# Retention and gated unit on one core: value weights behind a third unit of loads, first gated units a turn later, loads behind the stores

## Chip, cores and metric

The kernel runs on one core of a Trainium2 chip. The metric is the device time of one execution in microseconds (us), less is better. The five engines of the core are TensorE (PE), VectorE (DVE), ScalarE (ACT), GpSimd (POOL) and SyncE (SP); each works through its own instructions in order, and transfers between HBM and the on-chip memory SBUF are issued from the queues of SP, ACT or POOL.

## What is computed

A retention layer (attention without softmax, with a decay) feeds a gated unit: a causal convolution of five taps gives a gate, a projection gives values, and their product is projected again. There are 8 batches, 8 heads, 576 positions, 64 elements per head; everything is given and returned in float32.

```python
scores = q @ k.T / sqrt(64)                       # [8, 8, 576, 576]
ret = scores * gamma_h ** (s - t)                 # where s >= t, else 0
x = (ret @ v), heads side by side                 # [8, 576, 512]
gate = sigmoid(sum_k conv_w[k] * x[s - 4 + k])    # per channel
out = (gate * (x @ w_val)) @ w_out                # [8, 576, 512]
```

## The kernel before

The decay is split into a factor for the key's position (`gin`, put into v when it is cast to bf16) and one for the query's position (`gout`, put into the result), so that a state of 64x64 per head can be carried along the sequence instead of the full score matrix.

The work is cut into 18 units (`dcs`, L68 to L72): for each group of four batches eight "full" units of 256 positions (two per batch) and one "tail" unit that holds the last 64 positions of the four batches. Unit 8 and unit 17 are the tails. The loads of q, k and v for a full unit are one DMA of 512 KB each (L87); for a tail they are four DMAs of 128 KB each (L92), with pieces of 256 bytes, so twelve in all.

The main loop (L506) goes over m = 1 to 18. The order of instructions on each engine is written out by hand in it. Turn m does the scores, masks, state update and result of unit m, and beside it the later stages of earlier units: the convolution and gate of unit m-1 (`conv` L390, `gate` L405), the value projection of unit m-1 (`value` L410, in two halves i) and the output projection of unit m-2 (`project` L420, in two halves i). It also transposes q and k of unit m+1 (`turn`, copied from PSUM by ACT in `take_turned`, L271), casts k, q and v of unit m+2 to bf16 on GpSimd (L225, L241), and issues the loads of unit m+6. Unit 0 is done in a prologue (L451 to L501), where the loads of units 0 to 6, the weights and the masks are prepared as well.

What the steps below touch:

- Buffers for loaded q, k, v: four each (`ld`, LB = 4), so the load of unit m+6 needs the cast of unit m+2 done.
- `ob` (L426): the SBUF tile from which an output half is stored, five buffers. `project` copies PSUM to `ob` on ACT (L432) and issues the store on SP (L434). A copy waits until the store five copies ago has landed.
- `ps_g`: two PSUM banks that conv, value, project and others take in turn. A matmul into a bank waits until what was in it has been read.
- SP's queue holds nearly all loads and all stores in program order. In turn m: store of project(m-2, 0), loads of unit m+6, store of project(m-2, 1).
- Value weights `wvf` (L106): four DMAs of 256 KB, each into 64 of the 128 partitions (L112), issued after the loads of units 0 and 1. `prep_wv` (L213) casts them into the order of columns that `ORDER` (L121) gives, in two parts: part 1 on GpSimd in the prologue, part 0 on ACT in m=1.
- Output weights `wob` (L122): four DMAs from GpSimd's queue, each into 64 partitions, converted to bf16 on the way (L127).
- `dg`: four diagonals (one per block of channels) made by `prep_diagonals` (L209) from the convolution weights, which `prep_conv_weights` (L201) transposes into `cw`. All four are made on VectorE, at four places.
- `keep_warm` (L444): matmuls on zeros that keep TensorE occupied.

Of the kernel before, what the change touches and what calls it, by code (L numbers as in the profile page):

```python
# [21 lines left out]
def kernel(  # L22
# [57 lines left out]
    with tc.manual_schedule():  # L80
# [14 lines left out]
        def load(name, m):  # L95
            t = ld.tile([P, H, R, D], F32, name=f"f{name}")
            fetch(nc.sync, t, {"q": q, "k": k, "v": v}[name], m)
            loaded[name, m] = t

        cwn = consts.tile([KC * NP, P], F32, name="cwn")  # L100
        nc.scalar.dma_start(out=cwn, in_=moe_conv_w.rearrange("k (o i) -> (k o) i", i=P))
        for m in range(2):
            for name in "kqv":
                load(name, m)

        wvf = consts.tile([P, NP, DM], F32, name="wvf")  # L106
        wv_src = moe_w_val.rearrange("(op ob hl i) n -> ob hl i op n", ob=2, hl=2, i=HP)
        wv_dst = wvf.rearrange("p (op ob) n -> ob p op n", ob=2)

        def load_wv(eng, i):  # L110
            for ob in range(2):
                eng.dma_start(out=wv_dst[ob, half[i]], in_=wv_src[ob, i ^ ob])  # L112

        for i in range(2):
            load_wv(nc.sync, i)
        for m in range(2, LB):
            for name in "kqv":
                load(name, m)


        ORDER = ((0, 0, 1, 0), (HP, 0, 0, 1), (0, 2, 0, 0), (HP, 2, 1, 1))  # L121
        wob = consts.tile([P, NP, DM], BF16, name="wob")  # L122

        def load_wo():
            src = moe_w_out.rearrange("(pr ab hl p) n -> ab hl p pr n", pr=2, ab=2, hl=2)
            for (p0, blk, ab, hl) in ORDER:
                nc.gpsimd.dma_start(out=wob[p0:p0 + HP, blk:blk + 2, :], in_=src[ab, hl])  # L127


        zeros = consts.tile([P, DM], BF16, name="zeros")  # L130
# [4 lines left out]
                                compare_op=ALU.is_equal, fill=0.0)  # L135
        idb = consts.tile([P, HP], BF16, name="idb")
        nc.vector.tensor_tensor(idb, ident[:, 0:HP], ident[:, HP:P], op=ALU.add)
        toki = consts.tile([P, NCH + 1, R], mybir.dt.int32, name="toki")
        nc.gpsimd.iota(toki[:, 0:NCH], pattern=[[W, NCH], [1, R]], base=0, channel_multiplier=R)
        nc.gpsimd.iota(toki[:, NCH], pattern=[[0, R]], base=NCH * W, channel_multiplier=1)  # L140
# [42 lines left out]
            if pr == 1:  # L183
                nc.scalar.activation(gin, gin, AF.Exp)
        warm = consts.tile([P, 1], F32, name="warm")
        identf = consts.tile([32, 32], F32, name="identf")
        nc.vector.tensor_copy(identf, ident[0:32, 0:32])
        id2 = consts.tile([P, HP], F32, name="id2")
        nc.vector.tensor_copy(id2, idb)

        xg = [[xp.tile([P, GB, NP, PAD + (W if c < NCH else TAIL)], BF16, name=f"x{g}{c}") for c in range(NCH + 1)]
              for g in range(B // GB)]
# [8 lines left out]
        def prep_conv_weights():  # L201
            cps = spare(ps_g, "g")[:, 0:KC * NP]
            nc.tensor.transpose(cps, cwn, identf[0:KC * NP, 0:KC * NP])
            cps = cps.rearrange("p (k o) -> p k o", k=KC)
            nc.vector.tensor_copy(cw[:, :, 0::2], cps[:, :, 0::2])
            for i in range(2):
                nc.vector.tensor_copy(cw[half[1 - i], :, 1::2], cps[half[i], :, 1::2])

        def prep_diagonals(o, eng):  # L209
            eng.tensor_tensor(dg[:, o], cw[:, :, o].unsqueeze(2).to_broadcast([P, KC, HP]),  # L210
                              id2.unsqueeze(1).to_broadcast([P, KC, HP]), op=ALU.mult)
# [18 lines left out]
        def cast_k(m, *copies):  # L230
            cast("k", m, copies)
# [25 lines left out]
        def turn(which, m, bank=None):  # L257

            src = (kbf, qbf)[which][m]
            dst = new_bank() if bank is None else bank  # L260
            for pr in range(NP):
                for r in range(R):
                    nc.tensor.transpose(dst[:, pr, r, :], src[:, pr, r, :, :].rearrange("p i d -> p (i d)"), ident)  # L263
            return dst
# [125 lines left out]
        def conv(n):  # L390

            g = [ps_g.tile([P, 2, 2 * P], F32, name="g") for _ in range(2)][::-1]
            gps[n] = g
            gsb[n] = {}
            lists = [], []
            for pr in range(2):
                a, b = 2 * pr, 2 * pr + 1
                for kk in range(KC):
                    for bank, rows, blks in ((0, half[1], (b, a)), (1, half[0], (a, b))):
                        lists[bank].append([mm(g[bank][half[i], pr, :], lhsT=dg[rows, blks[i], kk, :],  # L400
                                               rhs=xs(n, rows, blks[i], kk), start=(pr == 0 and kk == 0),
                                               stop=(pr == 1 and kk == KC - 1)) for i in range(2)])
            return lists
# [37 lines left out]
        ok = lambda m: 0 <= m < ND  # L441
        v_copy, g_copy, s_copy = nc.vector.tensor_copy, nc.gpsimd.tensor_copy, nc.scalar.copy

        def keep_warm(n):  # L444

            t = ps_o.tile([P, NP, R, HP], F32, name="o0").rearrange("p o r n -> p (o r n)")
            for _ in range(n):
                nc.tensor.matmul(t, zeros[:, 0:P], zeros, start=True, stop=True)  # L448


        keep_warm(8)  # L451
        cast_k(0, (v_copy, 4))
        bank = turn(0, 0)
        take_turned(0, 0, bank, (v_copy, 4))
        cast_q(0)
        prep_conv_weights()
        prep_diagonals(0, nc.vector)
        keep_warm(3)
        bank = turn(1, 0, spare(ps_g, "g", [P, NP, R, P], BF16))
        take_turned(1, 0, bank, (s_copy, 2), (v_copy, 2))  # L460
# [4 lines left out]
        for m in range(LB, LB + 2):  # L465
            for name in "kqv":
                load(name, m)
        prep_wv(g_copy, 1)
        keep_warm(3)
        run(scores(0, 0))  # L470
        masks(0, 0, 0)
        masks(0, 0, 1)
# [3 lines left out]
        keep_warm(2)  # L476
        run(update(0, 0))
        take_state(0, 0)
        keep_warm(1)
        run(update(0, 1))  # L480
        take_state(0, 1)
        run(carried(0, 1))
        prep_diagonals(1, nc.vector)
        prep_diagonals(2, nc.vector)
        bank = turn(0, 1)
        take_turned(0, 1, bank)
        bank = turn(1, 1)
        take_turned(1, 1, bank)
        run(*values(0, 1))
# [2 lines left out]
        take_x(0, 0)  # L492
        take_x(0, 1)
        pass_on(0)
        for (name, f) in (("k", cast_k), ("q", cast_q)):
            f(2)
            load(name, LB + 2)
        load_wo()
        cast_v(2)
        load("v", LB + 2)  # L500
        prep_diagonals(3, nc.vector)  # L501

# [1 line left out]
        for m in range(1, ND + 1):  # L506
            now, nxt, last = ok(m), ok(m + 1), m == ND
            late = m < 4
            hi, lo = conv(m - 1)

            if now:
                run(scores(m, 0))
                masks(m, 0, 0)
                masks(m, 0, 1)
            if last:
                run(lo, hi)
                gate(m - 1, 1)
                gate(m - 1, 0)
            elif late:
                run(lo[0:8], hi[0:8])  # L520
                run(pairs(update(m, 0)), hi[8:10])
                take_state(m, 0)
                gate(m - 1, 0)
                run(pairs(update(m, 1)), lo[8:10])
                take_state(m, 1)
                gate(m - 1, 1)
                run(carried(m, 1))
            else:
                run(carried(m, 1))
                run(pairs(update(m, 1)), lo[0:2])  # L530
                take_state(m, 1)
                run(lo[2:10], hi[0:8])
                gate(m - 1, 1)
                run(pairs(update(m + 1, 0)), hi[8:10])
                take_state(m + 1, 0)
                gate(m - 1, 0)
            if now:
                run(scores(m, 1))
                masks(m, 1, 0)
                masks(m, 1, 1)  # L540

            if last:
                value(m - 1, 1, spare(ps_s, "s1"))
                value(m - 1, 0, spare(ps_s, "s0"))
                project(m - 2, 0)
                project(m - 2, 1)
                project(m - 1, 0, last=True)
                project(m - 1, 1, last=True)
                continue
            if m == 1:  # L550
                prep_wv(s_copy, 0)
                value(0, 1)
            if nxt:
                bank = turn(0, m + 1)
                take_turned(0, m + 1, bank)
            if m > 1:
                value(m - 1, 1)
                project(m - 2, 0)
            if ok(m + 2):
                for (name, f) in (("k", cast_k), ("q", cast_q), ("v", cast_v)):  # L560
                    f(m + 2)
                    if ok(m + 2 + LB):
                        load(name, m + 2 + LB)

            run(*values(m, 1))
            run(*values(m, 0))
            run(carried(m, 0))
            take_x(m, 0)
            take_x(m, 1)
            pass_on(m)  # L570

            if nxt:
                bank = turn(1, m + 1)
                take_turned(1, m + 1, bank)
            value(m - 1, 0)
            if m > 1:
                project(m - 2, 1)
            if m == 3:
                run(update(m + 1, 0))
                take_state(m + 1, 0)  # L580
# [28 lines left out]
```

## Time and profile before

The median of three executions is 169.4 us (169.35 to 171.46). The profiled execution took 172.7 us, and the span from its first to its last instruction is 171.0.

| engine | busy us | share of the span | instructions |
|---|---|---|---|
| PE (matmul) | 150.2 | 88% | 3378 |
| DVE | 102.7 | 60% | 189 |
| ACT | 91.6 | 54% | 149 |
| POOL | 77.3 | 45% | 87 |

HBM reads are 30.42 MB, writes 9.44 MB. Starts of some turns (first score matmul of unit m): m=1 at 15.98 us, m=2 at 26.82, m=3 at 36.33, m=4 at 44.76 (its first state update), m=5 at 52.85, m=6 at 62.41, m=12 at 114.60.

How to read the lines that follow below. In the page, PEclk and DMA give one digit for each of 40 equal slices of the span (4.3 us): the TensorE clock that was granted, and the busy share of the DMA engines, in tenths. In a timeline each line is start, duration, engine, line of the code, operation, output<-input, shape, count, and in brackets the idle time before it and what ended it. "SPq" is SP issuing a DMA: its time is that of the issue, not of the transfer. In a view of stretches each line is a stretch from:to, its length, the busy time of each engine with the number of instructions, the granted clock, the DMA share and GB/s.

### The profile page before, as it was taken

The numbers are of one execution on the slowest core, as the hardware profiler recorded it, in microseconds if no ns is written. First come the engines' busy times: TensorE is split into PE (matmuls) and PEld (weight loads), VectorE is DVE, ScalarE is ACT, GpSimd is POOL, SyncE is SP. The second block draws the span as 40 slices with busy tenths as digits, with TensorE's granted clock in tenths as the row PEclk, the third lists the DMA queues.
The fourth block names the chain that finished last, engine by engine and source line by source line (L and its number), as shares of the span: only waits on it lengthen the run. The fifth ranks groups of instructions, "written<-read, shape, count | busy, mean of one in ns | idle before, by whom it ended". The sixth has DMA issues, their size and how long they took to land.

```text
span 171.0 us, 7633 instructions
## 1 busy us (share of the span) xinstructions
PE 150.2 (88%) x3378; PEld 108.7 (64%) x3378; DVE 102.7 (60%) x189; ACT 91.6 (54%) x149; POOL 77.3 (45%) x87
## 2 busy tenths in 40 slices
PE   7895898799999967999899995899999999999970
PEld 2453776567777645767577854477877687776620
DVE  6569365475767744756467764356777776667220
ACT  4565355547566355565566645247576575642340
POOL 4374599487728190637910926044629170000000
PEclk9999579999999999999999999789999999999999
DMA  4999999999997899999999999997762211131134
GB/s 132 347 334 220 334 279 252 330 306 325 306 290 158 201 288 333 331 314 335 326 312 300 335 312 338 264 281 172 177 222 99 71 65 61 65 120 67 66 123 123
DMA packets 69054, 39.81 MB, mean 233 GB/s; under 512 B 14218, under 2 KB 63902, under 8 KB 69022
## 3 DMA queue, kind: packets, MB, share of 16 engines
q1 hardware_dynamic: 68256, 38.54, 76.7%
q0 software_dynamic: 576, 0.52, 1.9%
q8 instruction: 26, 0.43, 1.0%
q10 hardware_dynamic: 190, 0.27, 0.6%
q14 instruction: 6, 0.05, 0.1%
HBM read 30.42 MB, written 9.44 MB: 233 GB/s over the span
## 4 chain that ended last, share of the span: by engine, by line
PE 63%; DMA 13%; SPq 6%; issue 6%; DVE 5%; POOL 3%; ACT 2%; ACTq 0%; POOLq 0%; DVEq 0%
PE g L424 15%; PE g L414 14%; PE g L253 11%; PE tps L263 8%; PE o L308 6%; DMA fq<-in_q_dram 6%; SPq L92 5%; PE s L253 5%; DMA fv<-in_v_dram 4%; DMA fk<-in_k_dram 2%; POOL vb L241 2%; PE st L253 2%; DMA out_dram<-ob 2%; PE o L448 2%; DVE dg L210 1%
## 5 line engine op out<-in xcount | busy, mean ns | idle before, releaser
L294 DVE TENSOR_TENSOR p<-s,mask 128x512 bf16<-128x512 f32 x62 | 40.0, 686 | 24.0 <-PE s L253 24.0
L271 ACT COPY kq<-tps 128x1024 bf16<-128x1024 bf16 x34 | 34.6, 1018 | 18.0 <-PE tps L263 17.7
L424 PE MATMUL g<-wob,z 128*128 128x512 bf16 x144 | 37.4, 386 | 1.9 <-ACT ob L432 1.9
L414 PE MATMUL g<-x,wvb 128*128 128x256 bf16 x272 | 36.2, 277 | 0.2 <-ACT gate L407 0.2
L432 ACT COPY ob<-g 128x512 f32<-128x512 f32 x34 | 19.9, 585 | 30.8 <-PE g L424 24.3
L241 POOL TENSOR_TENSOR vb<-fv,gin 128x1024 bf16<-128x1024 f32 x18 | 34.4, 1914 | 2.5 <-DMA fv<-in_v_dram 2.5
L253 PE MATMUL g<-x,dg 64*64 64x256 bf16 x720 | 31.8, 280 | 1.2 <-DVE x L343 0.5
L343 DVE TENSOR_TENSOR x<-o,gout 128x512 bf16<-128x512 f32 x32 | 22.1, 743 | 14.5 <-PE o L308 14.5
L356 POOL COPY x<-x 128x16 bf16<-128x16 bf16 x16 | 3.2, 197 | 59.8 <-DVE x L343 51.8
L417 DVE TENSOR_TENSOR z<-gate,g 128x512 bf16<-128x512 f32 x34 | 23.4, 687 | 9.8 <-PE g L414 8.8
L414 PEld LDWEIGHTS <-wvb 128*128 128x128 bf16 x288 | 26.9, 99 | 3.6 <-issue 0.6
L407 ACT ACTIVATE gate<-g 128x512 f32<-128x512 f32 x36 | 21.3, 604 | 10.3 <-DVE p L294 6.4
L253 PEld LDWEIGHTS <-dg 64*64 64x64 bf16 x720 | 23.9, 108 | 4.0 <-issue 3.0
L424 PEld LDWEIGHTS <-z 128*128 128x128 bf16 x144 | 14.2, 99 | 12.5 <-issue 2.7
L225 POOL CAST qb<-fq 128x1024 bf16<-128x1024 f32 x18 | 18.8, 1042 | 5.5 <-DMA fq<-in_q_dram 5.5
L253 PE MATMUL s<-kq 64*64 64x128 bf16 (+1 forms) x560 | 16.4, 220 | 3.7 <-issue 3.0
L225 POOL CAST kb<-fk 128x1024 bf16<-128x1024 f32 x17 | 17.7, 1042 | 2.7 <-DMA fk<-in_k_dram 2.4
L253 PEld LDWEIGHTS <-kq 64*64 64x64 bf16 x576 | 11.8, 108 | 11.2 <-issue 10.4
L253 PE MATMUL st<-vb,kb 64*64 64x64 bf16 x512 | 14.1, 196 | 1.7 <-ACT sd L378 1.3
L308 PEld LDWEIGHTS <-vb 64*64 64x64 bf16 x576 | 8.8, 110 | 9.7 <-issue 9.5
L253 PEld LDWEIGHTS <-kb 64*64 64x64 bf16 x512 | 12.6, 112 | 3.4 <-issue 3.3
L308 PE MATMUL o<-p,vb 64*64 64x128 bf16 (+1 forms) x576 | 12.0, 222 | 1.9 <-issue 1.9
(67 smaller groups left out, 116.5 us busy)
## 6 DMA issues: line engine op xcount, KB each, us to landing
fk<-in_k_dram SPq DMA_DIRECT2D x16, 512.0 KB, 6.1
fq<-in_q_dram SPq DMA_DIRECT2D x16, 512.0 KB, 6.6
fv<-in_v_dram SPq DMA_DIRECT2D x16, 512.0 KB, 7.3
out_dram<-ob SPq DMA_DIRECT2D x32, 256.0 KB, 4.4
wvf<-in_moe_w_val_dram SPq DMA_DIRECT2D x4, 256.0 KB, 6.6
fk<-in_k_dram SPq DMA_DIRECT2D x8, 128.0 KB, 4.2
fq<-in_q_dram SPq DMA_DIRECT2D x8, 128.0 KB, 3.2
fv<-in_v_dram SPq DMA_DIRECT2D x8, 128.0 KB, 3.8
```

The source lines that it names most:

```text
L225: copy(t[:, o:o + n], src[:, o:o + n])
L241: eng.tensor_tensor(vbf[m][:, h:h + n], loaded["v", m][:, h:h + n], g[:, h:h + n].unsqueeze(3).to_broadcast([P, n, R, D]), op=ALU.mult)
L253: return lambda: nc.tensor.matmul(*a, skip_group_check=True, **kw)
L271: copy(kq[m][:, which, o:o + n], bank[:, o:o + n])
L294: nc.vector.tensor_tensor(p[:, :, 0:n], sps[m, r][i][:, :, 0:n], mask[dcs[m][0], r].unsqueeze(1).to_broadcast([P, NP, n]), op=ALU.mult)
L308: nc.tensor.matmul(o, start=key not in opened, stop=False, skip_group_check=True, **kw)
L343: nc.vector.tensor_tensor(xg[b // GB][c][:, b % GB, :, x0:x0 + P].rearrange("p o (n r) -> p o r n", r=R), ops[m, ab], gout[:, :, t0:t0 + P ...
L407: nc.scalar.activation(t, gps[n][i], AF.Sigmoid)
L414: nc.tensor.matmul(vps[:, j, :], lhsT=wvb[:, o, 2 * i + j, :], rhs=xs(n, slice(0, P), o, PAD), start=(j == 0 and o == 0), stop=(j == 1 and ...
L417: nc.vector.tensor_tensor(z, gsb[n][i], vps, op=ALU.mult)
L424: nc.tensor.matmul(o, lhsT=zsb[n, j // 2][:, j % 2, i * P:(i + 1) * P], rhs=wob[:, j, :], start=(j == 0), stop=(j == NP - 1))
L432: nc.scalar.copy(ob, o)
```

## The change

It changes the order in which data come and the order of the first turns:

- Loads of three units instead of two go ahead of the value weights.
- The value weights come as one DMA of 512 KB over 128 partitions and two of 256 KB over 64, the last of which ACT issues in the middle of the prologue (`load_wv_rest`). The output weights come as three DMAs over 128 partitions; `ORDER` and the order of the blocks in `conv` are changed to suit.
- The transposed convolution weights and the diagonals are made earlier, two of the diagonals on GpSimd. Groups of `keep_warm` matmuls are cut, moved and added; a group can now go to a bank of `ps_g`.
- GpSimd's part of `prep_wv` comes after the casts of unit 2, ACT's part in m=2.
- The first gated units are held back: m=1 has no value, m=2 has the values of units 0 and 1 and no project, m=3 has the value of unit 2 and both halves of project for units 0 and 1. From m=4 on, all is as before.
- In each turn the three loads of unit m+6 are issued at the end, after both stores.

It is meant to give the first turns the q, k and v that they need sooner, to fill the weights at full width, and to keep stores from being queued behind loads.

```diff
-        for m in range(2):
+        for m in range(3):
             for name in "kqv":
                 load(name, m)
...
-        def load_wv(eng, i):
-            for ob in range(2):
-                eng.dma_start(out=wv_dst[ob, half[i]], in_=wv_src[ob, i ^ ob])
-
-        for i in range(2):
-            load_wv(nc.sync, i)
-        for m in range(2, LB):
+        nc.sync.dma_start(out=wv_dst[0], in_=moe_w_val.rearrange("(op ob p) n -> ob p op n", ob=2, p=P)[0])
+        nc.sync.dma_start(out=wv_dst[1, half[0]], in_=wv_src[1, 1])
+
+        def load_wv_rest():
+            nc.scalar.dma_start(out=wv_dst[1, half[1]], in_=wv_src[1, 0])
+
+        for m in range(3, LB):
...
-        ORDER = ((0, 0, 1, 0), (HP, 0, 0, 1), (0, 2, 0, 0), (HP, 2, 1, 1))
+        ORDER = ((0, 0, 0, 1), (HP, 0, 1, 0), (0, 2, 0, 0), (HP, 2, 1, 1))
...
-            src = moe_w_out.rearrange("(pr ab hl p) n -> ab hl p pr n", pr=2, ab=2, hl=2)
-            for (p0, blk, ab, hl) in ORDER:
-                nc.gpsimd.dma_start(out=wob[p0:p0 + HP, blk:blk + 2, :], in_=src[ab, hl])
+            src = moe_w_out.rearrange("(pr n) m -> n pr m", n=2 * P)
+            nc.gpsimd.dma_start(out=wob[:, 0:2, :], in_=src[HP:HP + P])
+            for pr in range(2):
+                nc.gpsimd.dma_start(out=wob[:, 2 + pr, :], in_=src[:, pr].rearrange("(t p) m -> t p m", p=HP)[0::3])
...
-                    for bank, rows, blks in ((0, half[1], (b, a)), (1, half[0], (a, b))):
+                    for bank, rows, blks in ((0, half[1], (a, b)), (1, half[0], (a, b))):
...
-        keep_warm(8)
+        keep_warm(4)
+        prep_conv_weights()
+        keep_warm(4)
         cast_k(0, (v_copy, 4))
+        for o in range(2):
+            prep_diagonals(o, nc.gpsimd)
         bank = turn(0, 0)
         take_turned(0, 0, bank, (v_copy, 4))
         cast_q(0)
-        prep_conv_weights()
-        prep_diagonals(0, nc.vector)
+        prep_diagonals(2, nc.vector)
+        prep_diagonals(3, nc.vector)
...
-        prep_wv(g_copy, 1)
-        keep_warm(3)
+        keep_warm(2)
...
         take_state(0, 0)
+        load_wv_rest()
         keep_warm(1)
...
-        prep_diagonals(1, nc.vector)
-        prep_diagonals(2, nc.vector)
         bank = turn(0, 1)
         take_turned(0, 1, bank)
+        keep_warm(2, spare(ps_g, "g"))
         bank = turn(1, 1)
...
         pass_on(0)
-        for (name, f) in (("k", cast_k), ("q", cast_q)):
+        keep_warm(4, spare(ps_g, "g"))
+        for (name, f) in (("k", cast_k), ("q", cast_q), ("v", cast_v)):
             f(2)
             load(name, LB + 2)
+        prep_wv(g_copy, 1)
         load_wo()
-        cast_v(2)
-        load("v", LB + 2)
-        prep_diagonals(3, nc.vector)
...
-            if m == 1:
-                prep_wv(s_copy, 0)
-                value(0, 1)
             if nxt:
                 bank = turn(0, m + 1)
                 take_turned(0, m + 1, bank)
-            if m > 1:
-                value(m - 1, 1)
-                project(m - 2, 0)
+
+            if m == 2:
+                prep_wv(s_copy, 0)
+            for (f, n, i) in {1: (), 2: ((value, 0, 1), (value, 0, 0)),
+                              3: ((value, 2, 1), (project, 0, 0), (project, 0, 1))}.get(
+                                  m, ((value, m - 1, 1), (project, m - 2, 0))):
+                f(n, i)
             if ok(m + 2):
-                for (name, f) in (("k", cast_k), ("q", cast_q), ("v", cast_v)):
-                    f(m + 2)
-                    if ok(m + 2 + LB):
-                        load(name, m + 2 + LB)
+                cast_k(m + 2)
+                cast_q(m + 2)
+                cast_v(m + 2)
...
-            value(m - 1, 0)
-            if m > 1:
-                project(m - 2, 1)
+            for (f, n, i) in {1: (), 2: ((value, 1, 1), (value, 1, 0)),
+                              3: ((value, 2, 0), (project, 1, 0), (project, 1, 1))}.get(
+                                  m, ((value, m - 1, 0), (project, m - 2, 1))):
+                f(n, i)
+            for name in "kqv":
+                if ok(m + 2 + LB):
+                    load(name, m + 2 + LB)
```

More of the change, by code (lines that the diff above doesn't have):

```diff
@@ L137 @@
         nc.vector.tensor_tensor(idb, ident[:, 0:HP], ident[:, HP:P], op=ALU.add)
+        identf = consts.tile([32, 32], F32, name="identf")
+        nc.vector.tensor_copy(identf, ident[0:32, 0:32])
+        id2 = consts.tile([P, HP], F32, name="id2")
+        nc.vector.tensor_copy(id2, idb)
         toki = consts.tile([P, NCH + 1, R], mybir.dt.int32, name="toki")
@@ L185 @@
         warm = consts.tile([P, 1], F32, name="warm")
[L186 to L189, printed above, removed]
         xg = [[xp.tile([P, GB, NP, PAD + (W if c < NCH else TAIL)], BF16, name=f"x{g}{c}") for c in range(NCH + 1)]
@@ L442, with keep_warm @@
         v_copy, g_copy, s_copy = nc.vector.tensor_copy, nc.gpsimd.tensor_copy, nc.scalar.copy
-        def keep_warm(n):
-            t = ps_o.tile([P, NP, R, HP], F32, name="o0").rearrange("p o r n -> p (o r n)")
+        def keep_warm(n, t=None):
+            if t is None:
+                t = ps_o.tile([P, NP, R, HP], F32, name="o0").rearrange("p o r n -> p (o r n)")
             for _ in range(n):
                 nc.tensor.matmul(t, zeros[:, 0:P], zeros, start=True, stop=True)
-        keep_warm(8)
+        keep_warm(4)
+        prep_conv_weights()
+        keep_warm(4)
         cast_k(0, (v_copy, 4))
+        for o in range(2):
+            prep_diagonals(o, nc.gpsimd)
         bank = turn(0, 0)
```

## The prediction

> **What bounds the kernel now.** I read the page first (busy shares, the 40 slices), then the chain of waits in order of time, then the timelines of the single engines around the places where the chain leaves TensorE.
>
> ```profile
> PE 150.2 (88%) x3378; PEld 108.7 (64%) x3378; DVE 102.7 (60%) x189; ACT 91.6 (54%) x149; POOL 77.3 (45%) x87
> PEclk9999579999999999999999999789999999999999
> DMA  4999999999997899999999999997762211131134
> ```
>
> TensorE is busy 88% of the span, and DMA is full for the first 30 of 40 slices (to about 128 us). Two resources are thus near their limit for most of the time. The view of busy time by stretch, one stretch per turn m of the main loop (from the first score matmul of m to that of m+1), tells who sets the pace:
>
> ```profile
> core 0: us, PE busy (x), PEclk, DMA share, GB/s
> 15.98:26.82 10.84, 8.94 (x184) 0.69 1.07 297
> 26.82:36.33 9.51, 8.02 (x184) 1.00 1.13 292
> 36.33:44.76 8.43, 7.79 (x194) 1.00 1.09 322
> 44.76:52.85 8.09, 7.73 (x201) 1.00 1.00 273
> 52.85:62.41 9.56, 7.61 (x194) 1.00 0.80 201
> 62.41:71.03 8.62, 7.72 (x189) 1.00 1.08 329
> ...
> 102.66:114.60 11.94, 9.19 (x188) 0.86 1.00 303
> 114.60:122.04 7.44, 7.44 (x196) 1.00 0.77 176
> ```
>
> A turn costs 7.44 us of TensorE work, and late turns take just that: TensorE is the bound there. m=1 to m=6 take 10.84, 9.51, 8.43, 8.09, 9.56 and 8.62 us, 10.4 us over 6 x 7.44. This is all that a change at the start can win. (m=11, 102.66 to 114.60, holds a stop of 2.75 us and a half clock that the code has no reason for; the profiled execution took 172.7 us, the median is 169.4. So I work with differences at the start of m=6, 62.41 us, and add them to 169.4.)
>
> The 2.1 us lost in m=5 are the key. SyncE's timeline, ACT's and TensorE's there:
>
> ```profile
> 44.44 1.37 SPq L87 DMA_DIRECT2D fv<-in_v_dram  x1
> 45.90 1.75 SPq L434 DMA_DIRECT2D out_dram<-ob  x1
> 47.74 2.71 SPq L92 DMA_DIRECT2D fk<-in_k_dram  x4
> 50.55 4.10 SPq L92 DMA_DIRECT2D fq<-in_q_dram  x4
> 54.75 3.22 SPq L92 DMA_DIRECT2D fv<-in_v_dram  x4
> 58.07 1.04 SPq L434 DMA_DIRECT2D out_dram<-ob  x2
> ...
> 60.82 0.58 ACT L432 COPY ob<-g 128x512 f32<-128x512 f32 x1 [3.94 <-DMA out_dram<-ob]
> ...
> 61.45 1.02 PE L424 MATMUL g<-wob,z 128*128 128x512 bf16 x4 [1.95 <-ACT ob L432]
> ```
>
> The first store (45.90) is issued 13 us after its data were ready (the first `ob` copy on ACT starts at 32.19 us), because SyncE issues in order and is behind: each 512 KB load holds it about 1.4 us. Then come the 12 tail loads of unit 8, 10.3 us, and only then the second store. There are five `ob` buffers. The seventh copy, project(3,0), needs the buffer of the second store: issued 58.07, landed 60.74. ACT stands 3.94 us and TensorE 1.95.
>
> **What the Trainium skill says.** "SBUF — State Buffer", section "Door 1: The DMA port swizzle": partitions 0 to 63 reach only 8 of the 16 DMA ports. The trace agrees: full loads ran at 346 GB/s, the value weights, in halves of 64 partitions, at 226, and the stretch with the output weights (also halves) at 246.
>
> ```profile
> core 0: us, PE busy (x) PEld busy (x) DVE busy (x) ACT busy (x) POOL busy (x), PEclk, DMA share, GB/s
> 3.00:11.00 8.00, 7.34 (x62) 3.51 (x60) 4.38 (x18) 5.70 (x9) 4.00 (x3) 1.00 1.15 346
> 12.00:16.00 4.00, 2.34 (x77) 1.92 (x77) 4.00 (x5) 2.51 (x4) 2.11 (x2) 1.00 1.08 226
> 17.00:21.00 4.00, 3.27 (x87) 3.02 (x89) 1.44 (x3) 1.02 (x3) 2.31 (x4) 0.50 1.14 338
> 26.00:30.00 4.00, 3.33 (x118) 2.63 (x116) 2.13 (x5) 2.04 (x5) 4.00 (x4) 1.00 1.20 246
> ```
>
> "TensorE: Matmul & The Clock Gate", section "What's actually happening": after an idle window of some 3.4 us TensorE runs at half clock until it has been busy for about one such window. The trace agrees: the half clock at 17 to 21 us follows a thin stretch, and one lies after the 2.75 us stop in m=11. "DMA: Bandwidth & Descriptors", section "Issuing engines are not separate DMA queues": what ACT issues shares the same DMA engines. "SBUF — State Buffer", section "Who interferes with whom": a VectorE operation with two SBUF inputs blocks against GpSimd's reads. The trace agrees: one diagonal on VectorE took 0.47 us alone and 1.29 beside GpSimd's value cast.
>
> **The change part by part.**
>
> *Diagonals and cw earlier.* Diagonals 1 and 2 leave VectorE at 13.01 to 15.60 us, on the chain. But the matmuls that the following x operation needs end at 15.57 anyway, so this wins nothing. The new place costs 3 small copies ahead of cast_k(0), about 0.3 us, and two diagonals on GpSimd ahead of cast_q(0): 320 elements each, by the 1.9 us for 1024 of the value cast about 0.6 us each, in a time when GpSimd waits 3.7 us for q. 0 to +0.5 us.
>
> *Warm-up matmuls.* Two ahead of turn(1,1) lie in its 1.1 us of waiting. Four ahead of m=1 take 4 x 0.3 to 0.45 us: m=1 starts at about 17.2 instead of 15.98. They should spare the half clock (m=1 ran at 0.69), which cost about 2 us.
>
> *Values and projects held back.* A group of 8 value or 4 project matmuls takes 0.87 us. m=1 loses its two values: 7.44 - 4 x 0.87 + 0.8 for the update chain = 4.7, ending 21.9. m=2 has four values and no project: as m=3 before, 8.4, and 1.0 for the stop without releaser seen at 32.5: 31.3. m=3 has two values and four projects: 8.43 + 2 x 0.87 = 10.2, ending 41.5. m=4 as before 8.1: 49.6 instead of 52.85. The data are there: unit 2 now comes before the value weights, so some 3 to 4 us sooner, and unit 4's k landed at 32.4 before, wanted at about 34. **TensorE gains 3.2 us up to here.**
>
> *Loads behind the stores.* In m=2 there is now no project, so the 12 tail loads of unit 8 are queued on SyncE with no store ahead; the four projects of m=3 are behind them. **All stores now wait for the tail loads, the first one too.** The sixth `ob` copy, project(2,1) at the end of m=4, needs the first store's buffer. It is wanted at 49.6. When does it come? Unit 7's last load was issued by 45.81. Value weights at full width: the first 512 KB take 0.52/346 = 1.5 us instead of 0.52/226 = 2.3; with the share of a quarter on ACT 1.0 saved (0.8 to 1.6). Output weights: 4 us at 246 instead of 322 GB/s is 0.95 us; all or nothing of it may go, I take it all: together 2.0 (0.8 to 2.5). The first store's 1.84 us are no longer ahead of the tail loads. So these start at 43.9 and take 10.3, or 9.5 as the second set at 113.14: I take 10.0, end 53.9. The store lands 2.66 us later (58.07 to 60.74; over all stores 2.0 to 6.7): 56.6. Copy and hand-over 0.63: 57.2. Queued behind it on ACT are all its later copies and gates; TensorE stops at the second convolution bank of m=5, 0.7 us into that turn, and has 6.75 us left: m=6 at 64.0. It stood from about 50.3 to 57.2, two windows, so half clock follows for one to two windows and costs 1.7 to 3.4 us, I take 2.5: m=6 at **66.5 against 62.41, 4.1 later**.
>
> *Later.* Once these stores are through, stores are ahead of loads in each turn; the second wait for an `ob` buffer (68.97, 2.54 us on ACT) goes. Of 3.05 us that m=6 to m=10 lose over 5 x 7.44, I credit 1.0 (0 to 2). 169.4 + 4.1 - 1.0 = **172.5**. Nothing at the end of the kernel changes.
>
> **The rivals.**
> A, the queue is no obstacle: units 0 to 7 and the value weights are 13.6 MB, 39.4 us at the best rate of 346 GB/s, so in by 42.5; a landing follows its issue by some 6 us, the tail loads would go from 36.5 to 46.5, and the first store would land by 49.2, before it is wanted. Then m=5 takes about 7.9 and m=6 starts at 57.5, 4.9 sooner: **164.5**, faster. For it: dips in DMA rate at 21 to 25 and 45 to 48 us (272 GB/s) that the change might end. Against it: no row shows 346 sustained after 12 us.
> B, a short wait: the store lands at 53, little half clock (1.7): 53.6 + 6.75 + 1.7 = 62.1, no gain and no loss: **169**.
> C, a longer wait: 0.8 saved on weights, the tail loads 10.3, landing after 4.3 (the median of stores): copy done at 60.2, half clock 3.4: m=6 at 70.4; with the credit **176**.
>
> **How the numbers follow.** Forecast 0.50, A 0.18, B 0.18, C 0.14. The forecast's spread of 1.5 us lies on both sides of +2% (172.8), a little less of it above: slower 0.14 + 0.23 = 0.37, same 0.18 + 0.27 = 0.45, faster 0.18. The range goes from 166 (a wait of a few us less than B) to 176 (C).
>
> **What would show it.** The first store on SyncE after all 12 tail loads, near 54 us; the sixth `ob` copy released by a store, at 56 to 57; TensorE idle 5 us or more from about 50, PEclk about 0.5 after it; m=5 starting near 49.6. The forecast is wrong if the sixth copy does not wait, or if the tail loads are issued before about 38 us; the step on diagonals if m=1 starts before 15.5.

## The result and the profile after

The changed kernel takes 177.84 us (median; 176.72 to 180.02), the kernel before 169.38 in the same comparison: a ratio of 1.051, 95% interval 1.040 to 1.062. It is slower by 5%, 5.3 us more than the 172.5 forecast and outside the range of 166 to 176. (The profiled execution is the longest of the four, 180.02 us; the starts of its turns are used below as they stand.)

The page of the changed kernel:

```profile
PE 151.6 (85%) x3383; PEld 109.3 (61%) x3383; DVE 100.5 (56%) x187; ACT 91.8 (52%) x149; POOL 79.2 (44%) x88
PE   7778668989994059999999899599999999999970
PEclk9999955899999756999999999999999999999997
q0 software_dynamic: 2352, 0.53, 2.4%
```

TensorE has the same work (151.6 us busy instead of 150.2), but there is a hole in the 13th to the 15th slice, from about 55 to 65 us, and a low clock in the 14th to the 16th. The last line, the queue of GpSimd's DMAs, has 2352 packets. It carries the output weights alone, and the same bytes were 576 packets before. I come back to it.

Busy time of TensorE in the stretches from one turn m to the next, m=1 to m=6:

```profile
core 0: us, PE busy (x), PEclk, DMA share, GB/s
15.35:22.50 7.15, 4.86 (x169) 1.00 1.13 318
22.50:35.98 13.48, 11.59 (x192) 0.62 0.97 229
35.98:46.60 10.62, 9.87 (x209) 1.00 0.84 233
46.60:54.56 7.96, 7.61 (x202) 1.00 0.99 278
54.56:73.95 19.39, 10.32 (x193) 0.74 0.93 261
73.95:81.44 7.49, 7.49 (x186) 1.00 1.07 321
```

m=5, which took 9.56 us before, takes 19.39. m=6 starts at 73.95 instead of 62.41, 11.5 us later. From m=6 to the end this execution needs 104.25 us, the one before 108.59. Both hold a stop in m=11 that the code has no reason for: that turn took 9.95 us here and 11.94 before, where 7.44 is usual. SyncE, ACT and TensorE around m=5:

```profile
26.84 4.83 SPq L87 DMA_DIRECT2D fk<-in_k_dram  x1
31.76 4.32 SPq L87 DMA_DIRECT2D fq<-in_q_dram  x1
36.17 2.96 SPq L87 DMA_DIRECT2D fv<-in_v_dram  x1
...
50.22 4.64 SPq L92 DMA_DIRECT2D fk<-in_k_dram  x4
54.96 2.82 SPq L92 DMA_DIRECT2D fq<-in_q_dram  x4
57.87 2.63 SPq L92 DMA_DIRECT2D fv<-in_v_dram  x4
60.60 2.09 SPq L434 DMA_DIRECT2D out_dram<-ob  x4
...
63.90 0.59 ACT L432 COPY ob<-g 128x512 f32<-128x512 f32 x1 [9.96 <-DMA out_dram<-ob]
...
64.53 1.91 PE L253 MATMUL g<-x,dg 64*64 64x256 bf16 x30 [9.07 <-ACT ob L432]
```

The foretold wait is there: all stores are behind the twelve tail loads, the sixth `ob` copy waits 9.96 us for the first of them, TensorE stands 9.07 us at the second convolution bank of m=5, and half clock follows. But the first store goes out at 60.60, not near 54: the tail loads begin at 50.22 instead of 43.9. The first three lines say where that comes from. The loads of unit 5 held SyncE 12.4 us where 4.3 is usual. The DMA engines were busy at first and idle for the most part later (stretches of the changed kernel, the last two columns are DMA share and GB/s):

```profile
28.00:30.00 2.00, 0.50 1.14 257
35.00:37.00 2.00, 1.00 0.34 61
```

From 28 to 30 us their share is full, at 257 GB/s. From 35 to 37 us DMA moved 61 GB/s, at a third of its share, while SyncE had loads issued. More than half of the little that ran then was output weights (the first two lines; the other two, of the whole execution, give the time from issue to landing last):

```profile
q0 software_dynamic: 71, 0.07, 21.3%
q1 hardware_dynamic: 99, 0.05, 13.0%
...
wob<-in_moe_w_out_dram POOLq DMA_DIRECT2D x1, 256.0 KB, 6.3
wob<-in_moe_w_out_dram POOLq DMA_DIRECT2D x2, 128.0 KB, 14.1
```

The first output-weight DMA, with plain 128 partitions, landed in 6.3 us. The other two, whose source starts with a dimension of 2 (`[0::3]` of a view with t outermost), took 14.1, though each carries 128 KB. Before, each of four landed in about 6.5.

### The profile page after: what moved, and what is told of

Read it like the earlier page. It is cut to its first block, busy times and chain, and to the rows that moved or that the text cites. A ratio compares the mean times of both kernels' runs of the same rounds, so it can differ in the third digit from the quotient of the medians.

```text
span 178.2 us, 7638 instructions
## 1 busy us (share of the span) xinstructions
PE 151.6 (85%) x3383; PEld 109.3 (61%) x3383; DVE 100.5 (56%) x187; ACT 91.8 (52%) x149; POOL 79.2 (44%) x88
## 3 DMA queue, kind: packets, MB, share of 16 engines
q0 software_dynamic: 2352, 0.53, 2.4%
## 4 chain that ended last, share of the span: by engine, by line
PE 63%; DMA 16%; POOL 6%; issue 4%; DVE 3%; ACT 3%; SPq 1%; ACTq 0%; POOLq 0%
PE g L424 14%; PE g L414 13%; PE g L253 11%; PE tps L263 8%; PE o L308 6%; DMA fq<-in_q_dram 6%; PE s L253 5%; DMA fk<-in_k_dram 5%; DMA fv<-in_v_dram 4%; PE st L253 3%; POOL vb L241 2%; DMA out_dram<-ob 2%; SPq L92 1%; POOL kb L225 1%; POOL qb L225 1%
## 5 line engine op out<-in xcount | busy, mean ns | idle before, releaser
L294 DVE TENSOR_TENSOR p<-s,mask 128x512 bf16<-128x512 f32 x62 | 39.9, 686 | 35.2 <-PE s L253 35.2
L253 PE MATMUL g<-x,dg 64*64 64x256 bf16 x720 | 33.3, 286 | 10.8 <-ACT ob L432 9.3
L414 PE MATMUL g<-x,wvb 128*128 128x256 bf16 x272 | 37.5, 285 | 0.7 <-ACT wvb L216 0.5
L424 PE MATMUL g<-wob,z 128*128 128x512 bf16 x144 | 36.6, 381 | 0.0
L253 PEld LDWEIGHTS <-dg 64*64 64x64 bf16 x720 | 24.4, 111 | 14.2 <-issue 13.2
L414 PEld LDWEIGHTS <-wvb 128*128 128x128 bf16 x288 | 27.8, 102 | 4.9 <-ACT wvb L216 1.0
L424 PEld LDWEIGHTS <-z 128*128 128x128 bf16 x144 | 14.2, 99 | 10.9 <-issue 0.7
L253 PE MATMUL s<-kq 64*64 64x128 bf16 (+1 forms) x560 | 17.1, 225 | 4.4 <-issue 2.9
L253 PEld LDWEIGHTS <-kq 64*64 64x64 bf16 x576 | 12.2, 110 | 11.4 <-issue 10.9
L378 ACT CAST sd<-st 128x256 bf16<-128x256 f32 x24 | 8.9, 370 | 11.6 <-PE g L253 7.1
```

The costliest lines, as they stand in the source:

```text
L253: return lambda: nc.tensor.matmul(*a, skip_group_check=True, **kw)
L294: nc.vector.tensor_tensor(p[:, :, 0:n], sps[m, r][i][:, :, 0:n], mask[dcs[m][0], r].unsqueeze(1).to_broadcast([P, NP, n]), op=ALU.mult)
L414: nc.tensor.matmul(vps[:, j, :], lhsT=wvb[:, o, 2 * i + j, :], rhs=xs(n, slice(0, P), o, PAD), start=(j == 0 and o == 0), stop=(j == 1 and ...
L424: nc.tensor.matmul(o, lhsT=zsb[n, j // 2][:, j % 2, i * P:(i + 1) * P], rhs=wob[:, j, :], start=(j == 0), stop=(j == NP - 1))
```

## The experiments

Two theories. **Theory 1, the queue**: what is ahead of the first store on SyncE sets when TensorE goes on, and the output weights' two DMAs push it back. **Theory 2, the early turns**: the loads are late for the casts and TensorE's first turns are slow in themselves; the wait for `ob` only takes the place of that. Each run's time stands beside that of the kernel before on the same chip. These medians went from 169.3 to 170.6, but single executions of the kernel before from 165.9 to 173.6; differences of 1 to 2 us between kernels with few executions tell nothing. The changed kernel itself has only the four executions of the result, so a difference from its 177.84 us is one between comparisons.

### The two output-weight DMAs in another form

```diff
-            for pr in range(2):
-                nc.gpsimd.dma_start(out=wob[:, 2 + pr, :], in_=src[:, pr].rearrange("(t p) m -> t p m", p=HP)[0::3])
+            for t in range(2):
+                nc.gpsimd.dma_start(out=wob[half[t], 2:4, :], in_=src[3 * HP * t:3 * HP * t + HP])
```

> The changed kernel with only the output weights' second and third DMA changed: two DMAs with 64 partitions outermost, in place of two whose source starts with a dimension of 2. Theory 1 (these two run on few DMA engines, hold the loads of units 4 and 5 on those engines and so push the tail loads and the first store back): the load that held SyncE from 26.8 to 39.2 us falls to about 5 us, the first store goes out near 54 instead of 60.6, turn m=6 starts near 67.5 instead of 73.95, and the time is 171 to 173. Theory 2 (the loads are late because casts and buffers are late in the first turns): store still near 60, time 177 to 178.

Measured: 173.03 us (before: 170.64), 4.8 below the changed kernel. SyncE and ACT of this kernel:

```profile
26.66 5.16 SPq L87 DMA_DIRECT2D fk<-in_k_dram  x1
31.92 1.40 SPq L87 DMA_DIRECT2D fq<-in_q_dram  x1
33.41 1.40 SPq L87 DMA_DIRECT2D fv<-in_v_dram  x1
...
55.48 2.04 SPq L434 DMA_DIRECT2D out_dram<-ob  x4
...
58.58 0.58 ACT L432 COPY ob<-g 128x512 f32<-128x512 f32 x1 [6.05 <-DMA out_dram<-ob]
```

The loads of unit 5 take 8.1 us instead of 12.4 and the first store goes out 5.1 us sooner (I had expected 6.6: the first load of unit 5 is still held 5.16 us). m=6 starts at 67.3. These are nearly the forecast's own numbers (66.5 and 172.5): its path from the store to m=6 holds for the change with this one form of DMA repaired, though m=5 began at 53.1 us and not at 49.6.

### Ten output buffers

```diff
-    op_sb = ctx.enter_context(tc.tile_pool(name="osb", bufs=5))
+    op_sb = ctx.enter_context(tc.tile_pool(name="osb", bufs=10))
```

> The changed kernel with ten output buffers instead of five, so that no copy waits for the early stores; the order on the queues is unchanged. Theory 1 (the 10 us wait of the sixth output copy is the loss): m=6 starts near 62.5 instead of 73.95, no half clock at 65, time 165.5 to 167.5. Theory 2 (the load stream is the bound and the wait only stands in its place): TensorE waits for units 6 to 8 instead, time above 172.

Measured: 167.11 us (before: 170.64). The stretches of m=4, m=5 and m=6:

```profile
46.80:54.70 7.90, 7.44 (x199) 1.00 1.06 300
54.70:62.10 7.40, 7.29 (x191) 1.00 0.78 182
62.10:69.60 7.50, 7.39 (x187) 1.00 0.95 301
```

The first store goes out as late as in the changed kernel (60.28), and nobody cares: m=5 takes 7.40 us instead of 19.39 and TensorE waits for no load in its stead. The wait for a buffer, with the half clock after it, is the whole loss. Theory 2 falls as an explanation of the 8 us.

### Both edits

> Both edits on the changed kernel. Theory 1: the wait is gone and the turns m=2 and m=3 also lose less, as their casts no longer wait for stretched loads: 2 to 4 us under ten buffers alone, 162 to 165. If the stretched loads cost nothing beyond the store's date: the same as ten buffers alone, within 0.5 us.

> The same kernel as the earlier one with repaired output weights and ten output buffers, to stand beside the one with warm-up groups on the same chip: 166.5 to 168.5 us, m=6 from 61 us on.

Measured: 168.45 us (before: 170.64), and 167.92 (before: 169.66) on another chip, ratio 0.981, interval 0.965 to 0.997. Against ten buffers alone nothing is gained, where I had expected 2 to 4 us. m=6 starts at 61.2 (60.0 on the other chip) instead of 62.1. So the stretched loads cost about 1 us up to m=6 by themselves, and nothing of it shows in the time, where 168.45 stands beside 167.11 on the same chip; the rest of their cost was the date of the store.

### The kernel before with the same two DMAs

```diff
-            for (p0, blk, ab, hl) in ORDER:
+            for (p0, blk, ab, hl) in ORDER[0:2]:
                 nc.gpsimd.dma_start(out=wob[p0:p0 + HP, blk:blk + 2, :], in_=src[ab, hl])
+            src = moe_w_out.rearrange("(pr n) m -> n pr m", n=2 * P)
+            for pr in range(2):
+                nc.gpsimd.dma_start(out=wob[:, 2 + pr, :], in_=src[:, pr].rearrange("(t p) m -> t p m", p=HP)[0::3])
```

> The kernel before with only half of its output weights loaded by the two DMAs that start with a dimension of 2. Theory 1: they take 13 to 15 us to land instead of 6.5, the loads behind them and with them the tail loads and the second store move back by some 6 us (58.1 to 64), and the time rises to 173 to 176. Theory 2: 169 to 170.

Measured: 174.52 us (before: 170.64), the size expected, by another way. These DMAs land after up to 13.6 us, and in this kernel the projects of m=2 need them:

```profile
35.64 0.58 PE L427 MATMUL g<-wob,z 128*128 128x512 bf16 x1 [3.90 <-DMA wob<-in_moe_w_out_dram]
38.26 0.58 PE L427 MATMUL g<-wob,z 128*128 128x512 bf16 x1 [2.04 <-DMA wob<-in_moe_w_out_dram]
```

TensorE waits 5.9 us for the weights themselves, m=3 starts at 44.4 instead of 36.3, and the second store, 3.5 us later than before (61.56), meets no waiting copy any more. The form costs some 4 us here, through the weights, and some 5 in the changed kernel, through the store.

### Each of the two DMAs cut in two

```diff
-                nc.gpsimd.dma_start(out=wob[:, 2 + pr, :], in_=src[:, pr].rearrange("(t p) m -> t p m", p=HP)[0::3])
+                for c in range(2):
+                    m0 = c * DM // 2
+                    nc.gpsimd.dma_start(out=wob[:, 2 + pr, m0:m0 + DM // 2],
+                                        in_=src[:, pr, m0:m0 + DM // 2].rearrange("(t p) m -> t p m", p=HP)[0::3])
```

> The changed kernel with each of the two output-weight DMAs that start with a dimension of 2 cut into two by columns: four DMAs of the same form, twice as many packets of half the size, one more issue of about 0.8 us each on GpSimd. If such a DMA runs on two DMA engines only and the next takes the next two, four of them use eight engines: they land in 8 to 10 us instead of 13 to 15, and the first store goes out at 57 to 59 instead of 60.6. If the form costs by the packet, whatever the engines: landing 15 us or more, first store at 61 or later.

The Trainium skill, "DMA: Bandwidth & Descriptors", section "Rules for kernel authors", says that an outermost dimension below 16 confines a DMA to at most that many engines. If that were all, four such DMAs would use twice the engines and land sooner. Measured: 176.41 us (median of two; before: 169.34), no repair. The first store goes out at 60.45, and the view of DMA issues shows hardly faster landing, 13.4 us where it was 14.1:

```profile
wob<-in_moe_w_out_dram POOLq DMA_DIRECT2D x4, 64.0 KB, 13.4
```

The trace also records single packets. It does not name their engines, but it tells how many are under way at once. Of the output weights in the plain form there are up to 16 to 22 data packets in flight; of the two DMAs of this form in the changed kernel never more than 4 (5 in some of its variants, once the first DMA is through), of the four in this run never more than 8. This agrees with the skill's rule, two engines for each DMA, and the cut did spread the data: their last packet ended at 38.2 us, in the changed kernel at 39.9. It would explain the held loads too: from 35 to 37 us in the changed kernel at most 8 packets of the loads were in flight, where over 20 are usual, as if only their share on a few busy engines were left. That is argued from the counts and not shown.

But the form has another trace, packets of 4 bytes. Before, the output weights came with 64 of them for four DMAs (16 each); with the repaired form 48 for three; in the changed kernel 1840 for three; with the two cut in two 3664 for five. Each DMA of this form thus brings 912 of them, the others 16. In this run the last of them ended at 42.0 us, 3.8 us after the data; in the changed kernel they ended with the data, at 39.9. So few engines alone do not account for the landing, and how much of it is due to these packets is open. That the form costs is shown from both sides; why is shown only in part.

### Tail loads behind the stores of m=3

```diff
-            for name in "kqv":
-                if ok(m + 2 + LB):
-                    load(name, m + 2 + LB)
+            for n in {2: (), 3: (2 + 2 + LB, 3 + 2 + LB)}.get(m, (m + 2 + LB,)):
+                for name in "kqv":
+                    if ok(n):
+                        load(name, n)
```

> The changed kernel with one edit of order: in m=2 no loads are issued, and the tail loads of unit 8 go behind the four stores of m=3, just ahead of those of unit 9. Buffers and output weights stay as in the changed kernel. Theory 1 (what is queued ahead of the first store sets the restart): first store near 50 us, the sixth copy waits 1 us or not at all, m=6 starts at 62 to 63, time 166 to 168.5. Theory 2 (the loads themselves are the bound): what is won at the store is lost again waiting for units 8 and 9, time above 172.

Measured: 171.85 us, ratio 1.022 (1.010 to 1.034); expected 166 to 168.5, a miss. Order alone still takes 6 of the 8 us away: the first store goes out at 49.01 and m=6 starts at 62.0, both as expected. But the sixth copy waits 2 us, and I had not seen the second wait, of the tenth:

```profile
54.68 0.58 ACT L432 COPY ob<-g 128x512 f32<-128x512 f32 x1 [2.02 <-DMA out_dram<-ob]
...
72.64 0.58 ACT L432 COPY ob<-g 128x512 f32<-128x512 f32 x1 [3.77 <-DMA out_dram<-ob]
```

Now the tail loads and those of unit 9 stand between the stores of m=3 and of m=4. The next pair is issued at 65.31, and the tenth copy waits for it; half clock follows. A wait in an in-order queue moves to the next one who needs that queue.

### Values and projects not held back

```diff
+            if m == 1:
+                prep_wv(s_copy, 0)
+                value(0, 1)
...
-            for (f, n, i) in {1: (), 2: ((value, 0, 1), (value, 0, 0)),
...
+            if m > 1:
+                value(m - 1, 1)
+                project(m - 2, 0)
...
```

> The changed kernel with the value and project schedule of the kernel before (value of unit 0 in m=1, projects of unit 0 in m=2); all else as changed. The two stores of unit 0 are then ahead of the tail loads. Theory 1: the sixth and seventh copy do not wait, the eighth, at the end of m=5, waits for a store behind the tail loads (near 61 us, landed near 64), so m=6 starts at 64 to 66 and the time is 168 to 171. If holding back is harmless by itself: 177 to 178.

Measured: 175.84 us, ratio 1.044 (1.028 to 1.059); expected 168 to 171, a miss. No copy waits for a store any more, so that part is right, but other waits came that I had not looked for:

```profile
23.98 1.89 PE L414 MATMUL g<-x,wvb 128*128 128x256 bf16 x8 [2.83 <-POOL wvb L216]
...
37.80 0.38 PE L424 MATMUL g<-wob,z 128*128 128x512 bf16 x1 [2.62 <-DMA wob<-in_moe_w_out_dram]
40.42 0.59 PE L424 MATMUL g<-wob,z 128*128 128x512 bf16 x1 [2.24 <-DMA wob<-in_moe_w_out_dram]
```

With the value weights behind a third unit of loads, TensorE waits in m=1 for their cast on GpSimd, which itself waited for them to land, and in m=2 for the output weights, which are still in the slow form here. Holding back is the other half of loading the weights later: this run does not judge it alone.

### The kernel before, loads behind both stores

```diff
                     f(m + 2)
-                    if ok(m + 2 + LB):
-                        load(name, m + 2 + LB)
...
                 project(m - 2, 1)
+            for name in "kqv":
+                if ok(m + 2 + LB):
+                    load(name, m + 2 + LB)
```

> The kernel before with only the three loads of each turn moved behind its second store. Theory 1: both stores of unit 0 go ahead of the tail loads, so the seventh copy no longer waits; the eighth waits for the first store of unit 1, near 58 us, landed near 61, as the seventh did: m=6 starts at 61 to 63, time within 1.5 us of the kernel before. It is not this part of the change by itself that costs 8 us. Rival (late loads are the cost): 174 or more.

Measured: 170.02 us against 170.3, ratio 0.996 (0.988 to 1.003): no difference, as expected, but not by the way expected. The eighth copy did not wait: the longest wait of a copy for a store was 0.7 us, and m=6 starts at 61.3 instead of 62.4. By itself this part is harmless; it hurts only where a turn has loads and no store ahead of them, as m=2 has once its projects are held back.

### The kernel before with ten output buffers

> The kernel before with ten output buffers. Theory 1: the waits at 60.8 and 69.0 go, m=6 starts at 60.3 to 60.6 instead of 62.4, time 1.5 to 2.5 us under the kernel before. Rival (TensorE would wait elsewhere): no difference.

Measured: 166.05 us against 170.3, ratio 0.978 (0.974 to 0.982), more than the 1.5 to 2.5 us expected. m=5 takes 7.40 us instead of 9.56:

```profile
53.10:60.50 7.40, 7.29 (x191) 1.00 0.78 178
```

m=6 starts at 60.5, as expected. **This version beats both kernels**, with one number changed. But the earlier m=6 is only 1.9 of the 4.2 us. Moving the loads behind both stores took nearly all waits for stores away as well, and its time did not change. Where the rest of the gain comes from is open.

### More warm-up matmuls

```diff
+        def warm_up(n, i):
+            keep_warm(n, spare(ps_g, "g"))
...
-            for (f, n, i) in {1: (), 2: ((value, 0, 1), (value, 0, 0)),
+            for (f, n, i) in {1: ((warm_up, 3, 0),), 2: ((value, 0, 1), (value, 0, 0)),
...
-            for (f, n, i) in {1: (), 2: ((value, 1, 1), (value, 1, 0)),
+            for (f, n, i) in {1: ((warm_up, 5, 0),), 2: ((value, 1, 1), (value, 1, 0)),
```

> The changed kernel with repaired output weights, ten output buffers, and two groups of warm-up matmuls (3 and 5) in m=1, where the held-back values left TensorE waiting. If the half clock in m=2 (22.8 to 28.9 us) comes from the thin m=1: no half clock there, m=2 takes about 2 us less than the 12.6 us of the kernel without these groups, and the time is 1 to 2.5 us lower. If the half clock is not the reason for the long m=2 (the stop without releaser at 23 to 25 us and the wait for the cast of the value weights are): m=2 shorter by less than 1 us, time the same within 0.7 us.

Measured: 168.69 us (before: 169.66), ratio 0.989 (0.980 to 0.998), beside 167.92 without these groups. m=2 takes 11.3 us with them and 10.9 without. In this pair neither kernel had a half clock in m=2, so this pair does not tell what the half clock costs; the groups win nothing. The two profiles of the kernel without them do: on the first chip, with 3.4 us of half clock, m=2 took 12.6 us, and 10.9 on this one.

The kernel before with ten buffers and, of the change, the early diagonals and warm-up matmuls:

> The kernel before with ten output buffers and of the change only the early diagonals and the warm-up matmuls. If these parts of the change are worth what m=1 showed (no half clock from 17 to 24 us): m=6 starts 1 to 2.5 us before the 60.5 us of the kernel with ten buffers alone, and the time is 163.5 to 166, below both kernels. If the half clock only moves to m=2, as in the changed kernel: 166 to 167.5.

Measured: 166.53 us (before: 169.66), ratio 0.988 (0.977 to 0.998). m=6 starts at 59.3, 1.2 us before that of ten buffers alone, and the profile shows no half clock in the first turns, but the time is not lower than theirs.

## Why the prediction was wrong

**Bound and key.** Right. TensorE is the bound in steady turns; the place that decides is the `ob` buffer behind SyncE's queue. With ten buffers m=5 takes 7.40 us in both kernels.

**The wait.** Right in kind: the sixth copy, the second bank of m=5, the half clock. Wait and half clock came out as reckoned: from the TensorE restart at 64.53 to m=6 at 73.95 are 9.42 us, against 6.75 + 2.5 in the forecast.

**The date of the first store: the step that failed.** The forecast had "Output weights: 4 us at 246 instead of 322 GB/s is 0.95 us; all or nothing of it may go, I take it all", a gain from more partitions. In its place two of the three DMAs took twice as long to land, and with these two in another form the first store goes out at 55.48 instead of 60.60. So where the forecast had a saving of 0.95 us, this form put 5.1 us on the date of the first store. The prediction had bounded the term by nothing and a gain, and not by a loss. I read the destination (128 partitions) and not the source (a dimension of 2 in front). What is left of the 6.7 us between 53.9 and 60.6 is 1.6: with the other form the tail loads begin at 45.0 instead of 43.9 and take 10.5 us instead of 10.0. That one load of unit 5 still holds SyncE 5.16 us there fits the first part; why it does is open.

**TensorE's lead up to m=5.** Wrong, without consequence. m=1 was to start at 17.2 because of four more warm-up matmuls, and started at 15.35. By its own sign the step on diagonals, "this wins nothing", was wrong too, as m=1 starts before 15.5; but a single profile cannot say so. The start of m=1 differs from one profile to the next: 14.8 to 16.2 us in those of the kernel before and its variants, 15.3 to 16.6 in those of the changed kernel and its variants. They show neither a gain from the diagonals nor the 1.2 us for the warm-up. m=1 then was to take 4.7 us and has 4.86 us of work, but took 7.15: TensorE waits for masks, casts and copies, up to 1.10 us at once, and has no values to fill the gaps (read from the trace, not tested). The half clock was not spared but came later, 22.5 to 32.7 us instead of 16.9 to 23.7. So m=2 was to take 9.4 and took 13.48, at a mean clock of 0.62. In sum m=5 began at 54.56, 1.7 us later than before, not 3.2 earlier. The wait for the store swallowed it.

**The credit.** Right in kind: the second wait for an `ob` buffer is gone. Its size cannot be told. m=6 to m=10 took 37.75 us here and 40.25 before, more than the 1.0 us credited; but in the kernels with ten buffers, where no copy waits for a store, these turns took from 37.7 to 41.5 us.

**The sum.** m=6 came 7.5 us later than forecast: 6.7 from the issue of the first store, 5.1 of them by the form of the two DMAs, 0.6 from its landing (the copy starts 3.3 us after the issue; landing was taken as 2.66), 0.2 from the half clock. The median came 5.3 us later than forecast. The profiled execution is 2.2 us above the median, so the two cannot be matched more closely; that 172.5 plus 5.1 is 177.6, beside 177.84 measured, is in part luck. Of the rivals, C had the right direction for the wrong reasons. A and B are refuted: the sixth copy waited 9.96 us, where A had no wait and B a short one.

## What to carry to other kernels

An in-order queue that holds loads and stores has a date for each store, and this is reckoned from all that is ahead of it, not from when its data are ready. If a stage is moved later, ask which transfers are now ahead of its stores and which buffer comes free by them; more buffers are the cheaper cure where they fit. For a DMA, read the first dimension of both sides: here two DMAs that gathered 128 partitions through a source with a dimension of 2 in front landed in 14.1 us, two plain halves in 6.5.

## What the runs showed that was not expected

A DMA of GpSimd's queue whose source has a dimension of 2 in front brings 912 packets of 4 bytes instead of 16, lands in 14.1 us instead of 6.3 to 6.5, and holds up the loads of SyncE's queue: 61 GB/s over two microseconds with loads issued. Two such DMAs had at most 4 data packets in flight in the changed kernel. Cutting them into four of the same kind doubled that and left landing at 13.4 us. And of the change's many parts, none gave a gain in the whole that could be told apart, while doubling the number of output buffers is worth some 4 us on the kernel before: 166.05 us, beside 167.11 for the changed kernel with as many.
